# Experts' attention weights through DRAM: blocks of every fourth key, one transfer out and one back

## The chip, the cores and the metric

One core of one Trainium2 chip runs the whole program. The metric is the device time of one execution in microseconds; the median of three runs is compared. Beside the runs there is one profiled execution with a trace of every instruction. The engines are called PE (TensorE matmul), PEld (its weight loads), DVE (VectorE), ACT (ScalarE), POOL (GpSimd) and SP (SyncE, which here issues nearly all transfers).

## The reference

Three stages follow one another. The change touches the third alone.

```
attn_out = windowed attention with ALiBi over q, k, v             # B=4, H=8, S=576, D=64
x = transpose(attn_out) -> [4, 576, 512]
x = gated unit: relu(x @ w_in) -> u, v; v normalised, mixed over positions by w_spatial; (u * v) @ w_out
# third stage: mixture of 4 experts, each a causal attention of head size 64, top 2 of 4 by a gate
logits = x @ w_gate                    # [4, 576, 4]; softmax over the best two -> w
for e in range(4):
    q, k, v = x @ wq[e], x @ wk[e], x @ wv[e]
    scores = where(causal, -1e9, (q @ k.T) / 8)
    a = exp(scores - max); a /= a.sum(-1) + 1e-9
    ye = a @ v @ wo[e]
    out += (e is among the best two of this token) * w * ye
```

## The kernel before

**Tiling.** In the third stage a batch `b` (0 to 3) has 576 queries in five tiles `j`: four of 128 queries, and a tail (`j` = 4) of the last 64. For `j` below 4 the tile `(b, j)` holds 128 queries by the (j+1)·128 keys that they may see, for four experts `i`. For the tail, two experts stand in each half of the partitions, so that 64 queries fill 128 partitions; it sees all 576 keys. Positions are stored rolled by 64: columns 0 to 63 of the inputs are the tail's tokens, columns 64 to 575 the tokens 0 to 511.

**Steps of a tile.** The order of every step on every engine of the third stage is a list written out by hand, `THIRD`; the diff leaves it alone. Names in it are a kind and indices: `S` score matmuls into a PSUM bank pair (`scores_b`), `l` mask, scale and row minimum on DVE (`row_min`, which writes the tile's weights `p` in SBUF), `e` exponential and row sum on ACT, `f` the factors on DVE, `m` the scaling on POOL, `T` the turning of 32x32 blocks on DVE (`turn_blocks`, L1186), `w` the transfer of the turned weights to DRAM (`send`, L1193), `R` the transfer back (`read_back`, L1203), `A` the matmuls of values with turned weights (`attend_b`, L1239), `oh`/`ol` their removal from PSUM, `O` the output projection. `Q` and `qh`/`ql` are the projections of queries and keys and their removal, `V` and `vr` those of the values, `q4`/`k4` the tail's queries and keys in plain float32.

**Why DRAM.** Matmuls of values need the keys on the partitions. DVE turns each 32x32 block in place, so that after `T` the partition 32q + r holds, in block k, key 32k + r for the queries 32q to 32q + 31. What is left is a move of whole 32-row groups between partitions, and the way through DRAM does it. Before the change a block is 32 neighbouring keys: `send` issues four transfers, one for each group q of 32 partitions, in runs of 512 bytes (256 for the tail), into a DRAM tile ordered block, row, group. `read_back` then takes rows of 2048 bytes (1024 for the tail, in two transfers, of 128 and of 64 partitions). Three tiles, (3,2), (3,1) and (3,0), are turned on PE instead (`TURNED`).

**Buffers.** Banks for score pairs come from a pool of two (`psS`), all other PSUM banks from a pool of four (`psD`); a bank is free again when DVE's or ACT's last read of it has ended. `p` and the returned `pT` have three buffers each. Transfers of SP are issued in the order of its list, and each completion semaphore of eight is taken again only when the transfer that had it eight earlier has landed.

**Between the stages.** The masks `trit` (128 queries) and `tritail` (the tail) are made at the end of the second stage: POOL writes zeros, and SP loads the triangle beside them (L914 to L919). This stretch is not in a list by hand: the framework orders it by its own estimate of times. SP's list goes on there with the loads `st_wc` of the experts' weights `wcat` (L902) and `wt` (L957), from which PE makes the folded weights `W` for the third stage.

Of the kernel before, what the change touches and what calls it, by code (L numbers as in the profile page):

```python
# [10 lines left out]
F32 = mybir.dt.float32  # L11
BF16 = mybir.dt.bfloat16
# [6 lines left out]
ALU = mybir.AluOpType  # L19
# [3 lines left out]
B, H, S, D = 4, 8, 576, 64  # L23
P = 128
# [6 lines left out]
BIG = -float(2.0**40)  # L31
FAR = float(2.0**45)
FLT_MAX = 3.0e38
# [202 lines left out]
def block_kernel(ctx, tc, qP, kP, v, w_in, wspT, bsp, w_outT, wcat, wo, relt, tri, out):  # L236
    nc = tc.nc
# [10 lines left out]
    dram = ctx.enter_context(tc.tile_pool(name="dram", bufs=1, space=bass.MemoryType.DRAM))  # L248
# [663 lines left out]
    wB = ctx.enter_context(tc.tile_pool(name="wB", bufs=1, side="right", reuse_waits="tile"))  # L912
# [1 line left out]
    trit = wB.tile([P, 640], BF16, name="trit")  # L914
    nc.gpsimd.memset(trit[:, :512], 0.0)
    nc.sync.dma_start(trit[:, 512:640], tri[:, 0:128])
    tritail = wB.tile([P, S], BF16, name="tritail")
    nc.gpsimd.memset(tritail[:, :512], 0.0)
    nc.sync.dma_start(tritail[:, 512:576], tri[:, 128:192])  # L919
    tie = wB.tile([P, 1, E, E], F32, name="tie")  # L920
    nc.gpsimd.memset(tie, 0.0)
    for e in range(1, E):
# [91 lines left out]
    made = {}  # L1014

    def get(key, make):
        if key not in made:
            made[key] = make()
        return made[key]
# [11 lines left out]
    def values(b):  # L1031
        return get(("vt", b), lambda: wk.tile([P, 5, 260], F32, tag="vt", name=f"vt{b}"))
# [39 lines left out]
    def value_take(b, t):  # L1072
        pv = bank("pvB", b, t)
        if t < 4:
            nc.scalar.copy(values(b)[:, t, :], pv[:, :260])
        else:
            for o in range(2):
                nc.scalar.copy(values(b - 1 + o)[:64, 4, :], pv[64 * o : 64 * o + 64, :260])

    def gates(b, t0):  # L1080
        n = 1 if t0 else 4 + b % 2
# [25 lines left out]
    def tail_gate(b):  # L1107
        gt, gq = gate_of(b)
        for pr in range(2):
            nc.scalar.copy(gq[64 * pr : 64 * pr + 64, :], gt[0:64, 4, 2 * pr : 2 * pr + 2])  # L1110

    def keys_seen(j):
        return min(S, TOK[j][0] + P)
# [1 line left out]
    def score_bank(b, j, pr):  # L1115
        key = (b, j, 0 if j < 2 else pr)
        two = get(("psB", *key), lambda: psS.tile([P, 2, 512], F32, tag="S", name="psB%d_%d_%d" % key))
        return two[:, :, 256 * pr : 256 * pr + keys_seen(j)] if j < 2 else two

    def scores_b(b, j, at):  # L1120
        q0, kn = TOK[j][0], keys_seen(j)
        Q, K = heads(b, 0), heads(b, 1)
        if j == 4:
            view = score_bank(b, j, at)
            for c, k0, w in ((0, 64, 256),) if at == 0 else ((0, 320, 256), (256, 0, 64)):
                for pr in range(2):
                    for o in range(2):
                        r = slice(64 * o, 64 * o + 64)
                        nc.tensor.matmul(view[64 * pr : 64 * pr + 64, o, c : c + w], made["q4", b][r, pr, :], made["k4", b][r, pr, k0 : k0 + w], start=True, stop=True)
            return  # L1130
        for pr in (0, 1) if j < 2 else (at,):
            view = score_bank(b, j, pr)
            for n, (x_, y_) in enumerate(PASSES):
                for o in range(2):
                    r = slice(64 * o, 64 * o + 64)
                    nc.tensor.matmul(view[:, o, :kn], Q[x_][r, pr, 64 + q0 : 192 + q0], K[y_][r, pr, 64 : 64 + kn], start=(n == 0), stop=(n == 2))  # L1136

    def weights(b, j):
        n = 4 if j < 4 else 2
        p, st = get(("p", b, j), lambda: (wk.tile([P, 16 * P], F32, tag="p", name=f"pB{b}_{j}", bufs=3), wk.tile([P, 12], F32, tag="stat", name=f"stB{b}_{j}", bufs=4)))  # L1140
        if (b, j) in TURNED:
            return p, st, lambda i: p[:, i * (j + 1) * P : (i + 1) * (j + 1) * P], lambda t: t
        v = p[:, : (4 * (j + 1) if j < 4 else 18) * n * 32].rearrange("p (k e c) -> p k e c", e=n, c=32)
        return p, st, lambda i: v[:, :, i, :], lambda t: t.rearrange("p (k c) -> p k c", c=32)

    def row_min(b, j, i):
        p, st, part, cut = weights(b, j)
        V = nc.vector
        if j < 4:
            pr, o = divmod(i, 2)  # L1150
            q0, kn = TOK[j][0], keys_seen(j)
            V.tensor_tensor_reduce(part(i), cut(score_bank(b, j, pr)[:, o, :kn]), cut(trit[:, 512 - q0 : 512 - q0 + kn]), -0.125, FLT_MAX, ALU.add, ALU.min, st[:, i : i + 1])  # L1152
            return
        for n, (c0, w) in enumerate(((0, 256), (256, 320))):
            V.tensor_tensor_reduce(part(i)[:, c0 // 32 : (c0 + w) // 32], cut(score_bank(b, j, n)[:, i, :w]), cut(tritail[:, c0 : c0 + w]), -0.125, FLT_MAX, ALU.add, ALU.min, st[:, 8 + 2 * i + n : 9 + 2 * i + n])
        V.tensor_tensor(st[:, i : i + 1], st[:, 8 + 2 * i : 9 + 2 * i], st[:, 9 + 2 * i : 10 + 2 * i], op=ALU.min)

    def row_exp(b, j, i):
# [29 lines left out]
    def send(b, j):  # L1188
        p = weights(b, j)[0]
        n, w, e = sizes(j)  # L1190
        mid = get(("mid", b, j), lambda: dram.tile([16 if j < 4 else 18, 32, 4, w], F32, tag=f"mid{w}", name=f"mid{b}_{j}", bufs=3))
        for q in range(4):
            nc.sync.dma_start(mid[:n, :, q, :].rearrange("k i w -> i k w"), p[32 * q : 32 * q + 32, : n * w].rearrange("i (k w) -> i k w", w=w))  # L1193

    ready = {}

    def read_back(b, j):
        n, w, e = sizes(j)
        mid = made["mid", b, j]
        pT = wk.tile([P, 16 * P], F32, tag="pT", name=f"pTB{b}_{j}", bufs=3)  # L1200
        for c0, m, rows in ((0, n // 4, 128),) if j < 4 else ((0, 4, 128), (4, 1, 64)):
            src = mid[4 * c0 : 4 * c0 + rows // 32 * m].rearrange("(c k) i a w -> (k i) c (a w)", c=m)
            nc.sync.dma_start(pT[:rows, c0 * 4 * w : (c0 + m) * 4 * w].rearrange("i (c w) -> i c w", c=m), src)  # L1203
        full = pT[:, : (n + 3) // 4 * 4 * w].rearrange("p (c a e q) -> p c a e q", a=4, e=e, q=32)
        ready[b, j] = lambda pr, c, o: full[:, c, :, 2 * pr + o, :] if j < 4 else full[: 64 if c == 4 else 128, c, 2 * pr : 2 * pr + 2, o, :]

    homes = ["k0", "k1", "q0", "q1"]

# [22 lines left out]
    def attend_b(b, j):  # L1231
        qn = TOK[j][1]
        px = bank("pxB", b, j).rearrange("p (r c) -> p r c", r=4)
        vt, rhs = values(b), ready[b, j]
        for pr in range(2):
            for c in range(j + 1):
                kb = 64 if c == 4 else 128
                for o in range(2):
                    nc.tensor.matmul(px[64 * o : 64 * o + 64, pr, :qn], vt[:kb, c, (2 * pr + o) * 64 : (2 * pr + o) * 64 + 64], rhs(pr, c, o), start=(c == 0), stop=(c == j))  # L1239

    def take_b(b, j, part):
        qn = TOK[j][1]
# [35 lines left out]
    def act(name):  # L1278
        kind, rest_ = re.match(r"([a-zA-Z]+)(.*)$", name).groups()
        key = [int(k) for k in rest_.split(".")]  # L1280
        if kind in ("L", "GH", "GL", "BH", "BL"):
            load_g(name)
        elif kind == "VZ":
            nc.gpsimd.memset(values(*key)[64:128, 4, 256:260], 0.0)
        elif kind in ("qf", "kf"):
            whole(key[0], "qk".index(kind[0]), *key[1:])
        elif kind in ("qh", "ql"):
            project_take(*key, "hl".index(kind[1]))
        elif kind in ("oh", "ol"):
            take_b(*key, "hl".index(kind[1]))  # L1290
        elif kind == "g":
            get(("g", *key[:2]), lambda: gates(*key[:2]))[key[2]]()
        elif kind == "O":
            out_tile(*key[:2], key[-1], *key[2:-1])
        else:
            {"Q": project, "V": value, "vr": value_take, "h": tail_gate, "S": scores_b, "l": row_min, "e": row_exp, "f": factors, "m": scale, "T": turn_blocks,
             "w": send, "R": read_back, "t": turn_b, "c": turn_take, "A": attend_b, "oc": out_take, "o": out_store}[kind](*key)
# [11 lines left out]
def _tables():  # L1309
    import ml_dtypes  # L1310
    import numpy as np

    p = np.arange(128)[:, None]
    c = np.arange(256)[None, :]


    slope = -8.0 * 2.0 ** -(np.arange(H) + 1.0)[None, :, None]
    pair = [2 * np.arange(4) + (o ^ np.arange(4) % 2) for o in range(2)]
    tail = np.concatenate([slope[:, pair[o]] * ((p[:64] - c[:, :128]) % 128)[:, None, :] for o in range(2)], axis=0)
    tri = np.concatenate([np.where(c[:, :128] <= p, 0.0, BIG), np.where(c[:, :64] <= p % 64, 0.0, BIG)], axis=1)  # L1320
    return [t.astype(ml_dtypes.bfloat16) for t in (tail, tri)]


# [48 lines left out]
```

## Time and profile before

| | us |
|---|---|
| median of 3 runs (427.76 to 428.37) | 427.79 |
| profiled execution | 428.7 |
| span of its instructions | 426.8 |
| PE busy in the span | 411.0 |
| DVE busy | 316.6 |
| ACT busy | 243.1 |
| POOL busy | 171.2 |

The profiled execution has 1.9 us around its span, and is 0.9 us above the median. Its granted TensorE clock was 0.998 of full speed. The third stage begins at about 266 us of the span. A busy PE is not a PE at its peak: matmuls overlap, and their ends are modelled. Rows of a timeline or of a chain give start, length, and what ran; "[0.88 <-ACT u L780]" is idle time of the engine before the row and what ended it.

### The profile page before, as it was taken

To read this page: it belongs to the slowest core of one execution; us is meant where nothing else is said; L and a number is where in the kernel's file an instruction comes from. 1 tells how busy PE (TensorE), PEld (TensorE's weight loads), DVE (VectorE), ACT (ScalarE), POOL (GpSimd) and SP (SyncE) were. 2 spreads that over 40 slices of the span, in tenths; PEclk is the share of its full clock that TensorE was granted. 3 is DMA by queue.
4 is the path that set the end of the run, shared out by engine and by line. 5 is a ranking of instruction groups with operands and counts; after the bars stand their busy time and mean duration, and the time that the engine had idled before them with its cause. 6 is when DMAs were issued, how large, how long until landed. Compare 5 with 4: busy or idle time off the path is not lost.

```text
span 426.8 us, 12095 instructions
## 1 busy us (share of the span) xinstructions
PE 411.0 (96%) x4399; PEld 367.6 (86%) x4399; DVE 316.6 (74%) x1061; ACT 243.1 (57%) x757; POOL 171.2 (40%) x265
## 2 busy tenths in 40 slices
PE   6789999999999899999999999999999999999996
PEld 5567788799989798899898999999999998988885
DVE  5998999999899878787455422649888788678541
ACT  6898768756565455564245202656666557546642
POOL 3575553637406455432210000139665653544100
PEclk9999999999999999999999999999999999999999
DMA  8997366948855775331376160211879977798894
GB/s 249 382 298 287 101 170 206 293 127 259 274 171 134 220 231 156 90 104 39 118 256 263 49 223 2 63 50 26 217 198 282 248 160 244 214 270 219 204 279 126
DMA packets 76943, 80.06 MB, mean 188 GB/s; under 512 B 18002, under 2 KB 52946, under 8 KB 76500
## 3 DMA queue, kind: packets, MB, share of 16 engines
q1 hardware_dynamic: 76740, 79.15, 62.8%
q8 instruction: 35, 0.57, 0.6%
q14 instruction: 24, 0.20, 0.1%
q10 hardware_dynamic: 144, 0.13, 0.1%
HBM read 49.64 MB, written 29.62 MB: 186 GB/s over the span
## 4 chain that ended last, share of the span: by engine, by line
PE 77%; DMA 10%; DVE 4%; SPq 3%; ACT 3%; issue 1%; POOL 1%; DVEq 0%; POOLq 0%; ACTq 0%
PE pq L1042 12%; PE pu L777 10%; PE pg L792 9%; PE pv L714 9%; PE pvB L1070 6%; PE pxB L1239 6%; PE pout_None L1257 6%; PE psB L1136 4%; PE pw L946 4%; PE px L679 2%; DMA v<-in_v 2%; DMA carry<-p 2%; PE px L650 2%; DMA reltail<-in_relt 2%; DMA st_wc<-in_wcat 1%; DMA raw<-in_w_in 1%
## 5 line engine op out<-in xcount | busy, mean ns | idle before, releaser
L286 ACT ACTIVATE p<-p,st 128x128 f32<-128x128 f32 x144 | 56.5, 396 | 23.8 <-DVE st L285 19.3
L792 PE MATMUL pg<-wsp,vn 128*128 128x288 f32 x384 | 60.3, 297 | 0.9 <-ACT u L780 0.9
L777 PE MATMUL pu<-x,win 128*128 128x288 f32 x384 | 58.0, 297 | 0.2 <-DVE g L800 0.2
L714 PE MATMUL pv<-win,x 128*128 128x512 f32 x216 | 57.3, 398 | 0.3 <-ACT x L700 0.3
L792 PEld LDWEIGHTS pg<-wsp,vn 128*128 128x128 f32 x384 | 54.2, 188 | 3.4 <-ACT u L780 1.3
L565 POOL TENSOR_TENSOR p<-p,st 128x512 f32<-128x512 f32 (+1 forms) x28 | 32.4, 1162 | 60.9 <-DVE st L563 29.2
L1042 PE MATMUL pq<-x,W 128*128 128x288 f32 x384 | 56.8, 297 | 0.0
L777 PEld LDWEIGHTS pu<-x,win 128*128 128x128 f32 x384 | 53.4, 188 | 2.9 <-issue 1.0
L1042 PEld LDWEIGHTS pq<-x,W 128*128 128x128 f32 x384 | 52.5, 188 | 1.6 <-issue 0.8
L1160 ACT ACTIVATE pB<-pB,stB 128x128 f32<-128x128 f32 (+4 forms) x72 | 41.7, 581 | 13.8 <-DVE stB L1152 6.3
L298 POOL TENSOR_SCALAR pB<-pB,stB 128x384 f32<-128x384 f32 (+4 forms) x64 | 35.9, 580 | 28.8 <-DVE stB L1169 14.3
L714 PEld LDWEIGHTS pv<-win,x 128*128 128x128 f32 x216 | 38.4, 188 | 8.4 <-ACT x L700 1.2
L1152 DVE CUSTOM_DVE_ANT_0 pB<-psB,trit 128x128 f32<-128x128 f32 (+3 forms) x64 | 27.9, 485 | 6.0 <-PE psB L1136 5.7
L285 DVE CUSTOM_DVE_ANT_0 p<-ps,relm 128x128 f32<-128x128 f32 x128 | 30.1, 281 | 1.8 <-DMA carry<-p 1.7
L602 POOL TENSOR_SCALAR_AFFINE_SELECT pU<-pT 128x512 f32<-128x512 f32 (+1 forms) x26 | 18.8, 730 | 23.7 <-DMA pT<-carry 23.5
L1186 DVE STREAM_TRANSPOSE pB<-pB 128x1024 f32<-128x1024 f32 (+3 forms) x28 | 26.9, 980 | 1.9 <-POOL pB L298 1.7
L286 ACT ACTIVATION_READ_ACCUMULATOR p<-p,st 128x1 f32 x144 | 27.5, 191 | 0.0
L1070 PE MATMUL pvB<-W,x 128*128 128x260 f32 x192 | 27.1, 284 | 0.0
L1239 PE MATMUL pxB<-pTB,vt 128*64 128x128 f32 (+2 forms) x480 | 26.4, 260 | 0.0
L1257 PE MATMUL pout_None<-wo,o 128*128 128x512 f32 x102 | 26.3, 401 | 0.0
L1239 PEld LDWEIGHTS pxB<-pTB,vt 128*64 128x64 f32 (+1 forms) x480 | 23.2, 136 | 2.8 <-issue 1.1
L1070 PEld LDWEIGHTS pvB<-W,x 128*128 128x128 f32 x192 | 24.7, 188 | 0.8 <-issue 0.7
(195 smaller groups left out, 932.7 us busy)
## 6 DMA issues: line engine op xcount, KB each, us to landing
carry<-p SPq DMA_DIRECT2D x96, 64.0 KB, 2.4
pT<-carry SPq DMA_DIRECT2D x24, 256.0 KB, 3.1
q<-in_qP SPq DMA_DIRECT2D x20, 256.0 KB, 3.4
g_dram<-g SPq DMA_DIRECT2D x16, 288.0 KB, 3.8
gf<-g_dram SPq DMA_DIRECT2D x16, 288.0 KB, 4.8
raw<-in_w_in SPq DMA_DIRECT2D x8, 512.0 KB, 6.3
v<-in_v SPq DMA_DIRECT2D x16, 256.0 KB, 5.2
mid<-pB SPq DMA_DIRECT2D x16, 256.0 KB, 4.8
```

What stands on the lines that cost most here:

```text
L285: lambda: nc.vector.tensor_tensor_reduce(s_view, ps_view, tab, -0.125, FLT_MAX, ALU.add, ALU.min, nm),
L286: lambda: nc.scalar.activation(s_view, s_view, AF.Exp, bias=nm, scale=-1.0, accum_out=sm),
L298: nc.gpsimd.tensor_scalar(p, p, r, 0.0, op0=ALU.mult, op1=ALU.add)
L565: ops["m"] = lambda: nc.gpsimd.tensor_tensor(blocks, blocks, sm.unsqueeze(1).unsqueeze(3).to_broadcast([P, 4, n, 32]), op=ALU.mult)
L714: nc.tensor.matmul(pv, x[i][:, k, t0 : t0 + P], win[j][:, k, 512:1024], start=(n == 0 and k == 0), stop=(n == 2 and k == 3))
L777: nc.tensor.matmul(pu[:, :HALF], win[i][:, k, m * P : (m + 1) * P], x[j][:, k, c], start=(n == 0 and k == 0), stop=(n == 2 and k == 3))
L792: nc.tensor.matmul(pg[:, :HALF], vn[i][k][:, m * P : (m + 1) * P], wsp[j][:, k, c], start=(n == 0 and k == 0), stop=False)
L1042: nc.tensor.matmul(pq[:, :HALF], W[i][c0 // CUT][:, k, c0 % CUT : c0 % CUT + P], G[j][:, k, c], start=(n == k == 0), stop=(n == 2 and k == 3))
L1070: nc.tensor.matmul(pv[:, :260], rows, W[j][1][:, k, 512 - CUT :], start=(n == k == 0), stop=(n == 2 and k == 3))
L1160: nc.scalar.activation(part(i), part(i), AF.Exp, bias=st[:, i : i + 1], scale=-1.0, accum_out=st[:, 4 + i : 5 + i])
L1239: nc.tensor.matmul(px[64 * o : 64 * o + 64, pr, :qn], vt[:kb, c, (2 * pr + o) * 64 : (2 * pr + o) * 64 + 64], rhs(pr, c, o), start=(c == 0 ...
L1257: nc.tensor.matmul(po[:, : c.stop - c.start], o2[i][:, pr, :], wos[j][:, pr, c], start=(n == pr == 0), stop=(n == 2 and pr == 1))
```

## The change

A block becomes 32 keys of which each is four after the last (two in the tail), so that the partition of the returned tile is the row within the block times four (two) plus the block's residue. `send` is then one transfer of whole rows of the weights tile, and `read_back` one transfer (two for the tail) that takes, for each partition and group q, a run of (j+1)·512 bytes. For the tiles of 128 queries the reordering is made by `row_min`, which reads scores and mask in steps of four elements. For the tail it is made by `scores_b`, whose matmuls read the keys in steps of two elements, in 16 matmuls where there were 12. The tail's values move to the upper half of the partitions. The DRAM tiles get a tag for each `j` and four buffers.

```diff
-    tritail = wB.tile([P, S], BF16, name="tritail")
-    nc.gpsimd.memset(tritail[:, :512], 0.0)
-    nc.sync.dma_start(tritail[:, 512:576], tri[:, 128:192])
+    tritail = wB.tile([P, 2, 288], BF16, name="tritail")
+    nc.gpsimd.memset(tritail, 0.0)
+    nc.sync.dma_start(tritail[:, :, :32], tri[:, 128:192].rearrange("p (z i) -> p z i", z=2))
...  value_take
-                nc.scalar.copy(values(b - 1 + o)[:64, 4, :], pv[64 * o : 64 * o + 64, :260])
+                nc.scalar.copy(values(b - 1 + o)[64:, 4, :], pv[64 * o : 64 * o + 64, :260])
...  tail_gate
-            nc.scalar.copy(gq[64 * pr : 64 * pr + 64, :], gt[0:64, 4, 2 * pr : 2 * pr + 2])
+            nc.scalar.copy(gq[64 * pr : 64 * pr + 64, :], gt[64:128, 4, 2 * pr : 2 * pr + 2])
...  scores_b, j == 4
-            for c, k0, w in ((0, 64, 256),) if at == 0 else ((0, 320, 256), (256, 0, 64)):
+            for y, c, n in ((0, 0, 5), (1, 160, 4)):
                 for pr in range(2):
                     for o in range(2):
                         r = slice(64 * o, 64 * o + 64)
-                        nc.tensor.matmul(view[64 * pr : 64 * pr + 64, o, c : c + w], made["q4", b][r, pr, :], made["k4", b][r, pr, k0 : k0 + w], start=True, stop=True)
+                        keys = made["k4", b][r, pr, :].rearrange("p (g i z) -> p g i z", i=32, z=2)[:, y:9:2, :, at]
+                        to = view[64 * pr : 64 * pr + 64, o, c : c + 32 * n].rearrange("p (g i) -> p g i", i=32)
+                        nc.tensor.matmul(to, made["q4", b][r, pr, :], keys, start=True, stop=True)
...  weights
-        return p, st, lambda i: v[:, :, i, :], lambda t: t.rearrange("p (k c) -> p k c", c=32)
+        return p, st, lambda i: v[:, :, i, :], lambda t: t.rearrange("p (c z) -> p z c", z=4)
...  row_min, j == 4
-        for n, (c0, w) in enumerate(((0, 256), (256, 320))):
-            V.tensor_tensor_reduce(part(i)[:, c0 // 32 : (c0 + w) // 32], cut(score_bank(b, j, n)[:, i, :w]), cut(tritail[:, c0 : c0 + w]), ...)
+        for n in range(2):
+            V.tensor_tensor_reduce(part(i)[:, 9 * n : 9 * n + 9], score_bank(b, j, n)[:, i, :288], tritail[:, n, :], ...)
...  send
-        mid = get(("mid", b, j), lambda: dram.tile([16 if j < 4 else 18, 32, 4, w], F32, tag=f"mid{w}", name=f"mid{b}_{j}", bufs=3))
-        for q in range(4):
-            nc.sync.dma_start(mid[:n, :, q, :].rearrange("k i w -> i k w"), p[32 * q : 32 * q + 32, : n * w].rearrange("i (k w) -> i k w", w=w))
+        mid = get(("mid", b, j), lambda: dram.tile([P, n * w], F32, tag=f"mid{j}", name=f"mid{b}_{j}", bufs=B))
+        nc.sync.dma_start(mid, p[:, : n * w])
...  read_back
-        mid = made["mid", b, j]
+        src = made["mid", b, j].rearrange("(q i) (z c) -> (i z) q c", q=4, z=e)
-        for c0, m, rows in ((0, n // 4, 128),) if j < 4 else ((0, 4, 128), (4, 1, 64)):
-            src = mid[4 * c0 : 4 * c0 + rows // 32 * m].rearrange("(c k) i a w -> (k i) c (a w)", c=m)
-            nc.sync.dma_start(pT[:rows, c0 * 4 * w : (c0 + m) * 4 * w].rearrange("i (c w) -> i c w", c=m), src)
-        full = pT[:, : (n + 3) // 4 * 4 * w].rearrange("p (c a e q) -> p c a e q", a=4, e=e, q=32)
+        if j < 4:
+            nc.sync.dma_start(pT[:, : n * w].rearrange("p (q c) -> p q c", q=4), src)
+        else:
+            to = pT[:, : 20 * w].rearrange("p (q c) -> p q c", q=4)
+            nc.sync.dma_start(to[64:], src[:, :, : 5 * w])
+            nc.sync.dma_start(to[:64, :, w:], src[:, :, 5 * w :])
+        full = pT[:, : (n + 2 if j == 4 else n) * w].rearrange("p (a c e q) -> p c a e q", a=4, e=e, q=32)
...  attend_b: the tail's fifth chunk reads partitions 64 to 127 instead of 0 to 63, the same matmuls otherwise
```

## Rows read from the trace of the kernel before

**Rows 1.** Page, busy time: share of the span, instructions.

```profile
PE 411.0 (96%) x4399; PEld 367.6 (86%) x4399; DVE 316.6 (74%) x1061; ACT 243.1 (57%) x757; POOL 171.2 (40%) x265
```

**Rows 2.** Chain that ended last, 266 to 345 us, then 345 to 427: start, length, what.

```profile
by line: PE pq L1042 52.5%; PE pvB L1070 24.2%; PE psB L1136 11.3%; PE pxB L1239 8.1%; PE psB L1129 2.9%; PE pw L946 1.1%
...
305.65 1.14 PE psB L1129 x24
...
by line: PE pout_None L1257 30.4%; PE pxB L1239 23.4%; PE pq L1042 13.2%; PE psB L1136 10.7%; PE pvB L1070 9.8%; PE ptB L1218 3.2%; PE psB L1129 2.6%; PE pout L1257 1.7%; ACT ot L1265 0.5%; issue 0.0%; ACTq L1265 0.0%
...
417.49 2.34 PE pxB L1239 x48
```

**Rows 3.** Waits of SP's queue, 250 us to the end: us in total, times, longest.

```profile
SPq L1193 <- DVE pB L1186: 29.7, 9, 18.3
...
SPq L1203 <- DMA mid<-pB: 7.6, 8, 2.8
```

**Rows 4.** DMA issues: count, KB each, median us to landing.

```profile
mid<-pB SPq DMA_DIRECT2D x16, 256.0 KB, 4.8
...
pTB<-mid SPq DMA_DIRECT2D x7, 512.0 KB, 5.5
```

**Rows 5.** The DRAM tile's transfers on SP: duration ns min/median/max, first and last start.

```profile
L1193 SPq DMA_DIRECT2D mid<-pB x68: 303/492/3607, 294.3 to 404.1; - x68
L1203 SPq DMA_DIRECT2D pTB<-mid x21: 365/531/1682, 301.0 to 412.2; - x21
```

**Rows 6.** Timeline of SP near the end: start, length, what.

```profile
410.94 1.75 SPq L1203 DMA_DIRECT2D pTB<-mid  x2
```

**Rows 7.** Groups by line and form, DVE, third stage: busy us, mean ns.

```profile
L1152 DVE CUSTOM_DVE_ANT_0 pB<-psB,trit 128x512 f32<-128x512 f32 x16 | 10.3, 684 | 0.9 <-PE psB L1136 0.8
...
L1152 DVE CUSTOM_DVE_ANT_0 pB<-psB,trit 128x128 f32<-128x128 f32 x16 | 3.8, 286 | 0.4 <-PE psB L1136 0.3
```

**Rows 8.** One line of the first stage (word_ops "or"): duration ns min/median/max.

```profile
L440 DVE SCALAR_TENSOR_TENSOR u<-raw,u x8: 660/691/1385, 6.6 to 44.6; 128x512 int32<-128x512 int32 x8
```

**Rows 9.** Stretches of 10 us: busy PE, PEld, DVE, ACT, POOL, then clock and DMA.

```profile
290.00:300.00 10.00, 10.00 (x82) 9.17 (x79) 9.02 (x33) 5.64 (x19) 9.26 (x19) 1.00 0.22 45
...
320.00:330.00 10.00, 10.00 (x107) 9.07 (x104) 8.40 (x30) 6.33 (x21) 5.72 (x10) 1.00 0.99 287
...
350.00:360.00 10.00, 10.00 (x82) 8.65 (x80) 8.57 (x36) 7.86 (x26) 4.25 (x10) 1.00 0.93 261
```

**Rows 10.** The same stretches, DVE's instructions of L1152 alone.

```profile
290.00:300.00 10.00, 3.10 (x14) 1.00 0.22 45
...
320.00:330.00 10.00, 3.85 (x15) 1.00 0.99 287
...
350.00:360.00 10.00, 5.20 (x23) 1.00 0.93 261
```

**Rows 11.** A bank's way from DVE to PE: timelines of DVE and of PE.

```profile
303.30 0.42 DVE L263 TENSOR_TENSOR q<-pq,q 128x288 fp32r<-128x288 f32 x1
...
305.02 0.63 PE L1070 MATMUL pvB<-W,x 128*128 128x260 f32 x4
```

**Rows 12.** The tail's scores: L1129 in stretches (PE, PEld); then PE's groups, 306.16 to 306.19.

```profile
305.57:305.84 0.27, 0.26 (x4) 0.21 (x8) 1.00 1.03 273
...
L1129 PE MATMUL psB<-k,q 64*64 64x64 f32 x8 | 0.3, 217 | 0.0
```

**Rows 13.** Between the stages: timelines of SP, POOL and PE.

```profile
214.45 0.43 SPq L919 DMA_DIRECT2D tritail<-in_tri  x1
214.93 0.91 SPq L902 DMA_DIRECT2D st_wc<-in_wcat  x2
...
214.51 0.54 POOL L918 MEMSET tritail<- 128x512 bf16 x1
...
234.17 1.33 PE L792 MATMUL pg<-wsp,vn 128*128 128x288 f32 x8 [0.88 <-ACT u L780]
```

**Rows 14.** Chain that ended last, 226 to 250 us.

```profile
226.81 6.14 DMA st_wc<-in_wcat
```

More of the change, by code (lines that the diff above doesn't have):

```diff
@@ L1153, in row_min @@
             return
-        for n, (c0, w) in enumerate(((0, 256), (256, 320))):
-            V.tensor_tensor_reduce(part(i)[:, c0 // 32 : (c0 + w) // 32], cut(score_bank(b, j, n)[:, i, :w]), cut(tritail[:, c0 : c0 + w]), -0.125, FLT_MAX, ALU.add, ALU.min, st[:, 8 + 2 * i + n : 9 + 2 * i + n])
+        for n in range(2):
+            V.tensor_tensor_reduce(part(i)[:, 9 * n : 9 * n + 9], score_bank(b, j, n)[:, i, :288], tritail[:, n, :], -0.125, FLT_MAX, ALU.add, ALU.min, st[:, 8 + 2 * i + n : 9 + 2 * i + n])
         V.tensor_tensor(st[:, i : i + 1], st[:, 8 + 2 * i : 9 + 2 * i], st[:, 9 + 2 * i : 10 + 2 * i], op=ALU.min)
@@ L1198, in read_back @@
         n, w, e = sizes(j)
-        mid = made["mid", b, j]
+        src = made["mid", b, j].rearrange("(q i) (z c) -> (i z) q c", q=4, z=e)
         pT = wk.tile([P, 16 * P], F32, tag="pT", name=f"pTB{b}_{j}", bufs=3)
-        for c0, m, rows in ((0, n // 4, 128),) if j < 4 else ((0, 4, 128), (4, 1, 64)):
-            src = mid[4 * c0 : 4 * c0 + rows // 32 * m].rearrange("(c k) i a w -> (k i) c (a w)", c=m)
-            nc.sync.dma_start(pT[:rows, c0 * 4 * w : (c0 + m) * 4 * w].rearrange("i (c w) -> i c w", c=m), src)
-        full = pT[:, : (n + 3) // 4 * 4 * w].rearrange("p (c a e q) -> p c a e q", a=4, e=e, q=32)
-        ready[b, j] = lambda pr, c, o: full[:, c, :, 2 * pr + o, :] if j < 4 else full[: 64 if c == 4 else 128, c, 2 * pr : 2 * pr + 2, o, :]
+        if j < 4:
[5 more added lines that the diff above has]
+        full = pT[:, : (n + 2 if j == 4 else n) * w].rearrange("p (a c e q) -> p c a e q", a=4, e=e, q=32)
+        ready[b, j] = lambda pr, c, o: full[:, c, :, 2 * pr + o, :] if j < 4 else full[64 if c == 4 else 0 :, (c + 1) % 5, 2 * pr : 2 * pr + 2, o, :]
     homes = ["k0", "k1", "q0", "q1"]
@@ L1236, in attend_b @@
             for c in range(j + 1):
-                kb = 64 if c == 4 else 128
+                kb = slice(64 if c == 4 else 0, P)
                 for o in range(2):
-                    nc.tensor.matmul(px[64 * o : 64 * o + 64, pr, :qn], vt[:kb, c, (2 * pr + o) * 64 : (2 * pr + o) * 64 + 64], rhs(pr, c, o), start=(c == 0), stop=(c == j))
+                    nc.tensor.matmul(px[64 * o : 64 * o + 64, pr, :qn], vt[kb, c, (2 * pr + o) * 64 : (2 * pr + o) * 64 + 64], rhs(pr, c, o), start=(c == 0), stop=(c == j))
     def take_b(b, j, part):
@@ L1283, in act @@
         elif kind == "VZ":
-            nc.gpsimd.memset(values(*key)[64:128, 4, 256:260], 0.0)
+            nc.gpsimd.memset(values(*key)[0:64, 4, 256:260], 0.0)
         elif kind in ("qf", "kf"):
@@ L1319, in _tables @@
     tail = np.concatenate([slope[:, pair[o]] * ((p[:64] - c[:, :128]) % 128)[:, None, :] for o in range(2)], axis=0)
-    tri = np.concatenate([np.where(c[:, :128] <= p, 0.0, BIG), np.where(c[:, :64] <= p % 64, 0.0, BIG)], axis=1)
+    tri = np.concatenate([np.where(c[:, :128] <= p, 0.0, BIG), np.where(2 * (c[:, :64] % 32) + c[:, :64] // 32 <= p % 64, 0.0, BIG)], axis=1)
     return [t.astype(ml_dtypes.bfloat16) for t in (tail, tri)]
```

## The prediction, made before the changed kernel ran

> **What bounds the kernel now.** I read the busy times first, then the chain of work that ended last, then the waits of SP's queue, and last the groups of instructions that the diff touches. The busy times name PE, 411.0 of 426.8 us [rows 1]. An average hides stages, so the chain decides: from 266 to 345 us it consists of PE rows alone, and from 345 to the end of PE rows but for half a per cent [rows 2]. No transfer of the weights stands in it, in either stretch. The reader is to see there that the third stage is as long as PE's list of matmuls, and that a change in it is worth what it adds to or takes from that list, plus any wait that it brings up into it.
>
> SP's queue does wait, 29.7 us for DVE's turned blocks and 7.6 us for the weights to land in DRAM before they are fetched [rows 3]. That is time in which SP has nothing else ready to issue. It would count if PE waited for what is fetched, so the distance between fetch and use is the next thing to look at. The tightest is the last tile, (3,4): its two fetches are issued from 410.94 us on in 1.75 us [rows 6], the larger form of such a fetch lands after 5.5 us in the median [rows 4], so about 416.5 us, and the stretch of matmuls that opens with its own begins at 417.49 [rows 2]. There is about 1 us to spare in the worst place. Faster transfers make that 1 us larger and give PE nothing.
>
> **Transfers.** 17 tiles are sent with 4 issues each, 68 in all, with a median of 492 ns on SP [rows 5]; 51 go away, some 25 us of SP's time. The write changes from runs of 512 and 256 bytes to whole rows, the read from 2048 bytes to (j+1)·512. Packets fall for j = 3 from 2048 + 512 to 128 rows + 512, and for j = 0 stay at 640. So landing gets shorter, by an unknown part of the 4.8 us that a quarter of the largest tile takes [rows 4]. Worth on the path: 0, because PE's list covers it, at the tightest by the 1 us above. If a new transfer were longer than the old by more than that, PE would stop at the last tile by the rest; with the same bytes in fewer issues I see no ground for that.
>
> **Row minima, tiles of 128 queries.** 13 tiles keep this way, 52 instructions of L1152, with the same columns; what changes is that scores in PSUM are read in steps of four floats (16 bytes) and the mask in steps of 8 bytes. [...] No instruction before the change reads PSUM in such steps. The nearest row is L440, which reads SBUF in steps of two words (8 bytes) with 512 columns: 691 ns [rows 8], against 684 for 512 columns read without gaps. Lower bound: nothing. Upper bound: each column costs twice. [...] I take nothing, since the one strided row cost nothing, and keep the other end as a rival.
>
> [...]
>
> **Tail, row minima.** Two instructions of 256 and 320 columns become two of 288, now read without gaps: 576 columns either way. 0.
>
> **Tail, scores.** The columns stay 576 for each expert; three pieces become four, so a batch has 32 records where it had 24 (each float32 matmul shows as two). A batch takes 1.14 us now [rows 2]. Upper bound, if a record costs the average whatever its length: 8 · 1.14/24 = 0.38 us a batch, 1.5 us for four. Lower bound: nothing, if columns alone count. The rows are near the lower: four records of 256 columns, which run together, fill 0.27 us before a fifth begins, while all eight records of 64 columns are under way together with later ones [rows 12], so short records follow at a small part of the average. I take 0.1 us for four batches. This is on PE's list, with nothing to hide it. The keys are also read in steps of 8 bytes. Nothing on PE did that before; the bounds are nothing and a doubling of the four batches, 4 · 1.14 = 4.6 us. L440's row says that 8 bytes cost DVE nothing, and I take nothing, with the doubling as a rival.
>
> **Values of the tail, its gates, the zeroed columns.** The same instructions on other partitions: 0. The returned tile is read by `attend_b` in runs of 32 as before: 0.
>
> **The tail's mask.** Before, POOL zeroed 512 columns while SP loaded 64 others; the load was issued at 214.45 us, inside POOL's 214.51 + 0.54 [rows 13]. Now the load goes into the zeroed columns and has to wait for POOL, till about 215.1 us. What stands behind it in SP's list are the loads `st_wc` and `wt`, and a later `st_wc` stands in the chain with 6.14 us [rows 14]; PE idles 0.88 us before 234.17 us because of it [rows 13]. So this small edit lies closer to the path than the transfers do. If SP's order stays, everything behind moves by 215.15 - 214.45 = 0.7 us, and so does PE. If the framework, which orders this stretch by its own estimate, lets the two `st_wc` go first, they start 0.48 us earlier, and PE gets up to that back. Two ends, +0.7 and -0.5; I see no row that leans to either and take their middle, +0.1.
>
> **Sum.** 0 + 0 + 0.1 + 0.1 = +0.2 us. The profiled execution would go from 428.7 to 428.9; it stands 0.9 above the median of the runs, so in the runs' terms 427.79 + 0.2 = 428.0, from 427.2 to 428.6 with the two ends of the mask's wait and some of the tail's.
>
> **Rivals.** *DVE reads PSUM at half speed in steps of 16 bytes* (slower). Of an instruction of 512 columns, 0.53 of 0.684 us are columns, 0.78 of it, which doubling adds once more: 2.4 us to 290-300, 3.0 to 320-330, 4.1 to 350-360 [rows 10]. DVE has 9.02, 8.40 and 8.57 of 10 us taken there [rows 9], so it overruns by 1.4, 1.4 and 2.7 us, and the stretches in between are too full to recover the first. A bank that PE wants at 305.02 us was freed by DVE at 303.72 [rows 11]: 1.3 us of slack, and DVE's lag passes it from about 300 us on. PE then waits for banks. The overruns sum to 5.5 us; slack takes some off, the crowding of minima within a stretch adds some; I put it at 6, so 434. It decides as soon as a column costs more than about half as much again, since up to there the lag stays within the slack. For it: the largest of DVE's loads lie in the tightest stretches. Against it: 8 bytes cost nothing.
>
> *PE reads keys at half speed in steps of 8 bytes* (slower): up to +4.6 us, 0.2 with it, so about 432. Four tail batches would show it at once, and nothing else.
>
> *The mask's load moves behind `st_wc` and the lighter SP queue brings up more* (faster): at the most the whole idle 0.88 us before 234.17, so 426.9. For it: PE does idle there for a transfer. Against it: only the first transfers move, by 0.48.
>
> *The transfers don't get shorter at all*: 428.0 too, as nothing on the path waits for them.
>
> **How the numbers follow.** For this kernel 0.2% (0.86 us) is about what a measurement tells from no change. No change, 427.2 to 428.6: 0.50. DVE at half speed, 430.5 to 436, likeliest 434: 0.27. PE at half speed, 430 to 432.5: 0.13. Faster, 426.5 to 427: 0.10. The first gives "same"; the second and third "slower", 0.40; the fourth "faster". The predicted time is the likeliest, 428.0. A range that leaves out no more than 2 in 10 has to take in both slower cases in part: 427.0 to 434.5 holds 0.50 + 0.13 + about 0.18. The likeliest case's own range is 427.2 to 428.6.
>
> **What the profile after would show.** Row minima of 512 columns near 684 ns confirm the first step; near 1,200 they show the rival, with PE waiting for banks from 300 us on. A tail batch of 1.1 to 1.2 us confirms the second; 2 us the rival. SP's issue of the tail's mask at 215.1, or behind `st_wc`, settles the third, and PE's idle before its matmuls near 234 us says what it cost. Sends should be 17, and the fetch of (3,4) should land more than 1 us before its matmuls. What would make the prediction wrong is a strided read that costs more than the one at 8 bytes, or a wait in the third stage that no view of the kernel before shows.

## The result, and the profile after

The changed kernel takes 430.58 us in the median of four runs (430.28 to 431.4), the kernel before 428.02 in four runs beside it: a ratio of 1.0062 with a 95% interval from 1.0045 to 1.008. A second comparison, of 12 runs with 23 (`after_again` below), gives 1.0046 [1.0028, 1.0065]. It is slower by about 2 to 2.6 us. The time lies inside the range of 427.0 to 434.5, but the likeliest case was "no change", and that did not come. The profiled execution takes 430.81 us and its span is 428.8, at a granted clock of 0.999.

The busy times on the page answer to [rows 1]:

```profile
PE 410.8 (96%) x4431; PEld 368.2 (86%) x4431; DVE 316.6 (74%) x1061; ACT 243.6 (57%) x757; POOL 169.3 (39%) x265
```

PE has 32 records more (four batches with 8 each) and is busy for 410.8 us against 411.0, although the span is 2.0 us longer. So the loss is idle time of PE. DVE is busy for the same 316.6 us, so the row minima did not become slower. The groups of the row minima on DVE (line, form, then busy us and mean ns of one) answer to [rows 7]:

```profile
L1154 DVE CUSTOM_DVE_ANT_1 pB<-psB,trit 128x512 f32<-128x512 f32 x16 | 10.4, 685 | 0.8 <-PE psB L1138 0.8
...
L1154 DVE CUSTOM_DVE_ANT_1 pB<-psB,trit 128x128 f32<-128x128 f32 x12 | 2.8, 285 | 0.3 <-PE psB L1138 0.3
```

685 and 285 ns stand against 684 and 286. The transfers, as DMA issues with KB each and median us to landing, answer to [rows 4]; SP's issues of the sends (ns min/median/max) to [rows 5]:

```profile
mid<-pB SPq DMA_DIRECT2D x4, 1024.0 KB, 4.8
...
pTB<-mid SPq DMA_DIRECT2D x4, 1024.0 KB, 6.1
...
pTB<-mid SPq DMA_DIRECT2D x4, 320.0 KB, 6.4
```

```profile
L1194 SPq DMA_DIRECT2D mid<-pB x17: 319/325/390, 296.0 to 402.5; - x17
```

One transfer of 1 MB lands in the 4.8 us that a quarter of it took before. The packets of the whole program fall from 76,943 to 53,854, by the page. The chain from 266 to 345 us and from 345 us on still consists of PE's rows; the tail's scores in it, and the last matmuls that wait for a fetch, answer to [rows 2] and [rows 6]:

```profile
307.32 1.19 PE psB L1131 x30
...
340.27 1.19 PE psB L1131 x32
...
392.45 1.20 PE psB L1131 x31
...
419.35 2.34 PE pxB L1243 x48
```

```profile
411.61 0.58 SPq L1206 DMA_DIRECT2D pTB<-mid  x1
```

A batch of tail scores takes 1.19 us instead of 1.14. Of the last tile's two fetches the larger is issued at 411.61 us; each of its kind landed after 6.4 us, so it lands at 418.0, 1.3 us ahead of its matmuls. The smaller is issued at 412.25 and lands, by the median of its own kind (6.1 us), about 1.0 us ahead of them.

Then PE's waits from 205 to 262 us, between the stages. First the kernel before, then the changed one (us in total, times, longest):

```profile
PE pg L792 <- ACT u L780: 0.9, 1, 0.9
```

```profile
PE pv L714 <- DVE g L800: 2.3, 1, 2.3
```

That is the place of the loss. The wait of [rows 13] before 234 us is gone, and a longer one has come, for a gate product `g` on DVE. The timelines of SP and of DVE show how:

```profile
214.31 0.33 SPq L916 DMA_DIRECT2D trit<-in_tri  x1
214.69 0.91 SPq L902 DMA_DIRECT2D st_wc<-in_wcat  x2
215.64 0.43 SPq L919 DMA_DIRECT2D tritail<-in_tri  x1
```

```profile
218.82 0.96 DVE L263 TENSOR_TENSOR wc<-st_wc,wc 128x772 fp32r<-128x772 f32 x1 [1.81 <-ACT wc L266]
219.71 0.45 DVE L800 TENSOR_TENSOR g<-u,pg 128x288 f32<-128x288 f32 x1
```

The same stretch of DVE in the kernel before:

```profile
216.69 0.45 DVE L800 TENSOR_TENSOR g<-u,pg 128x288 f32<-128x288 f32 x1
218.93 2.07 DVE L263 TENSOR_TENSOR wc<-st_wc,wc 128x772 fp32r<-128x772 f32 x2 [1.79 <-ACT wc L266]
```

The framework let the two `st_wc` go ahead of the tail's mask, and in the same stroke it put the step of the folding that needs them (`wc`, the low part of a chunk) ahead of `g` on DVE. DVE ran them in that order: `g`, which ran at 216.69 us before, waits for `wc`, which waits for ACT's cast of the same chunk, which waits for the transfer. By the kernel `g` is the last to read its PSUM bank, and the banks that PE's next matmuls `pv` need come from the same pool; so PE stops. The chain of the changed kernel runs through it:

```profile
214.69 3.25 DMA st_wc<-in_wcat
217.96 0.84 ACT wc L266
218.82 0.96 DVE wc L263
219.78 0.38 DVE g L800
220.21 1.19 PE pv L714 x4
```

POOL's zeroing of `trit` begins between 211.62 and 214.29 us in the profiles of this study, a spread that arises ahead of what the change touches. So I compare stretches that begin there and last to the end of the span. It starts at 214.05 us before and at 214.29 after:

```profile
214.05 0.53 POOL L915 MEMSET trit<- 128x512 bf16 x1 [4.55 <-PE py L679]
```

```profile
214.29 0.53 POOL L915 MEMSET trit<- 128x512 bf16 x1 [4.15 <-PE py L679]
```

Before: 426.8 - 214.05 = 212.75 us. After: 428.8 - 214.29 = 214.51, so 1.76 more. PE's waits account for 2.3 - 0.9 = 1.4 of it and the tail's scores for 4 · 0.05 = 0.2; 0.16 are left without a name, less than two profiles of one kernel differ by.

### The profile page after: what moved, and what is told of

Same layout as the page of the kernel before. It is cut to its first block, busy times and chain, and to the rows that moved or that the text cites. A ratio compares the mean times of both kernels' runs of the same rounds, so it can differ in the third digit from the quotient of the medians.

```text
span 428.8 us, 12019 instructions
## 1 busy us (share of the span) xinstructions
PE 410.8 (96%) x4431; PEld 368.2 (86%) x4431; DVE 316.6 (74%) x1061; ACT 243.6 (57%) x757; POOL 169.3 (39%) x265
## 2 busy tenths in 40 slices
DMA packets 53854, 80.04 MB, mean 187 GB/s; under 512 B 8098, under 2 KB 29986, under 8 KB 52900
## 4 chain that ended last, share of the span: by engine, by line
PE 74%; DMA 13%; ACT 4%; DVE 4%; SPq 2%; issue 1%; POOL 0%; DVEq 0%; ACTq 0%
PE pq L1042 12%; PE pg L792 9%; PE pu L777 9%; PE pv L714 7%; PE pvB L1070 6%; PE pxB L1243 6%; PE pout_None L1261 6%; PE psB L1138 4%; PE pw L946 4%; DMA carry<-p 3%; DMA raw<-in_w_in 3%; DMA v<-in_v 2%; PE px L679 2%; ACT p L286 2%; DMA k<-in_kP 2%; PE pg L795 2%
## 5 line engine op out<-in xcount | busy, mean ns | idle before, releaser
L602 POOL TENSOR_SCALAR_AFFINE_SELECT pU<-pT 128x512 f32<-128x512 f32 (+1 forms) x26 | 17.4, 678 | 25.2 <-DMA pT<-carry 25.1
L1154 DVE CUSTOM_DVE_ANT_1 pB<-psB,trit 128x512 f32<-128x512 f32 (+3 forms) x52 | 23.6, 501 | 1.9 <-PE psB L1138 1.9
```

## Experiments

Times of the kernel before differ a little between sets of runs, so each ratio is to its own. The ratio is the recorded one and not the quotient of two medians. "Stretch" is the time from the zeroing of `trit` to the end of the span, in the one profiled execution. Two profiles of the same kernel differ there by 0.24 to 0.53 us (the changed kernel and `after_again`, the two of `before_mask_waits`, the two `late_fold` runs), so differences of 0.2 us in that column show nothing by themselves.

| run | median us | ratio to before [95%] | stretch us | PE's waits, 205 to 262 us |
|---|---|---|---|---|
| kernel before | 427.39 to 428.02 | | 212.75 | 0.9 for `u` |
| changed kernel | 430.58 | 1.0062 [1.0045, 1.008] | 214.51 | 2.3 for `g` |
| mask_apart | 427.81 | 1.0003 [0.9991, 1.0014] | 212.98 | 0.9 for `u` |
| before_mask_waits | 429.50 | 1.005 [1.0029, 1.0071] | 214.27 | 2.2 for `g` |
| fold_low_on_pool | 430.12 | 1.0059 [1.0037, 1.0082] | 216.21 | 2.4 for `u` |
| four_sends | 427.53 | 0.9996 [0.9978, 1.0014] | 212.68 | 0.8 for `u` |
| masks_later | 427.58 | 1.0003 [0.9987, 1.0018] | 212.61 | 0.5 for `g` |
| late_fold_on_pool | 426.88 | 1.0001 [0.9986, 1.0017] | 211.91 | none |
| tail_keys_in_order | 427.54 | 1.001 [0.9993, 1.0027] | 212.82 | 0.9 for `u` |
| minima_in_order | 427.44 | 1.0002 [0.9987, 1.0016] | 213.18 | 0.9 for `u` |
| late_fold_again | 427.18 | 0.9984 [0.9967, 1.0002] | 212.44 | 0.3 for `u` |
| before_late_fold | 426.28 | 0.9966 [0.9951, 0.998] | 211.78 | none |
| after_again | 429.50 | 1.0046 [1.0028, 1.0065] | 214.75 | 2.0 for `g`, 0.4 for `u` |
| before_mask_waits_again | 429.66 | 1.005 [1.0029, 1.0071] | 214.58 | 2.1 for `g`, 0.5 for `u` |

The theory was that the whole loss comes from one line, the zeroing of the tail's mask, by way of the order that the framework then chooses. The rivals were that the layout costs (transfers, strided reads), and that the wait of the mask's load costs as such.

**mask_apart.** The changed kernel, with POOL's zeros kept off the columns that SP loads:

```diff
-    nc.gpsimd.memset(tritail, 0.0)
+    nc.gpsimd.memset(tritail[:, :, 32:], 0.0)
```

> The changed kernel, but POOL zeroes only the columns of the tail's mask that the load does not fill, so the load waits for nothing. Theory: the loss arises between the stages, because the waiting load lets the framework put a step of the weights' folding ahead of a gate product on DVE; with the wait gone that order returns and the time is that of before plus the tail's scores, 428.0 + 0.2 = 428.2 us, with PE's idle before its matmuls near 234 us back at 0.9. Rival: the loss lies in the new layout of the third stage (strided reads, new transfers); then the time stays at 430.6.

The loss is gone. SP, DVE and PE's waits are as they were before the change:

```profile
213.24 0.33 SPq L916 DMA_DIRECT2D trit<-in_tri  x1
213.62 0.43 SPq L919 DMA_DIRECT2D tritail<-in_tri  x1
214.09 0.95 SPq L902 DMA_DIRECT2D st_wc<-in_wcat  x2
```

```profile
215.86 0.45 DVE L800 TENSOR_TENSOR g<-u,pg 128x288 f32<-128x288 f32 x1
218.34 2.02 DVE L263 TENSOR_TENSOR wc<-st_wc,wc 128x772 fp32r<-128x772 f32 x2 [2.04 <-ACT wc L266]
```

All of the change but this line costs about 0.2 us of the stretch (212.98 against 212.75), which is within the scatter, and nothing that the runs can tell.

**before_mask_waits.** The reverse: the kernel before, with nothing but the zeroing changed, so that its load must wait too.

```diff
-    nc.gpsimd.memset(tritail[:, :512], 0.0)
+    nc.gpsimd.memset(tritail, 0.0)
```

> The kernel before, with one word changed: POOL zeroes all 576 columns of the tail's mask, so the load into the last 64 has to wait for it. Nothing of the layout or the transfers changes. Theory: it loses what the changed kernel lost between the stages, 1.4 to 2.4 us, 429.4 to 430.4 us, and DVE again turns to the folding before the gate product at about 217 us. Rival (the layout is the cause): 428.0, no change.

The loss is there without any part of the layout, by the same order on DVE:

```profile
217.83 0.96 DVE L263 TENSOR_TENSOR wc<-st_wc,wc 128x772 fp32r<-128x772 f32 x1 [1.68 <-ACT wc L266]
218.71 0.45 DVE L800 TENSOR_TENSOR g<-u,pg 128x288 f32<-128x288 f32 x1
```

Its stretch is 1.52 us longer than before, against the changed kernel's 1.76. The two runs settle that the one line is enough for the loss, and that the loss goes with it.

**four_sends.** `mask_apart` with four sends for each tile, in whole rows of 32 partitions:

```diff
-        nc.sync.dma_start(mid, p[:, : n * w])
+        for q in range(4):
+            nc.sync.dma_start(mid[32 * q : 32 * q + 32], p[32 * q : 32 * q + 32, : n * w])
```

> The version with the mask's load free of the wait, but each tile goes to DRAM in four transfers of 32 partitions as before the change, in the new layout. Theory: transfers are covered by PE's list, so this is within 0.3 us of that version with one transfer, about 428.2. Rival: the single transfer saves something on PE's way, and four cost 0.5 us or more.

The time is that of `mask_apart` as far as the runs can tell, and so are the stretch and PE's wait. One issue instead of four is worth nothing here that shows.

**fold_low_on_pool.** The changed kernel, with the low parts of the two chunks of the folding that are loaded first made on POOL, so that DVE has nothing to wait for.

```diff
-        return lambda: split(wc[0][k], wc[1][k], raw_[k])
+        def halves():
+            nc.scalar.copy(wc[0][k], raw_[k])
+            lo_part(wc[1][k], raw_[k], wc[0][k], nc.gpsimd if k >= 2 else nc.vector)
+        return halves
```

> The changed kernel with its waiting mask, but the low parts of the two weight chunks that are loaded first are made on POOL and not on DVE. Theory: what cost time is that a gate product stood on DVE behind a step that waited for a transfer; with that step off DVE the product runs at about 217 us again, PE's wait of 2.3 us for it goes, and the time is 427.3 to 428.3. Rival that the waiting transfers themselves delay PE, not the order on DVE: 430 or more. Rival that the layout is the cause: 430.6.

This missed. `g` is early again, at 215.53 us, and PE's wait for it is gone; but PE now waits 2.4 us for `u`. The chain from 214 to 236 us says why:

```profile
222.29 6.70 DMA gf<-g_dram
229.08 0.40 ACT both L990
...
230.00 0.32 ACT u L780
...
231.54 0.96 PE pu L777 x4
```

ACT stands at `both`, a cast of the next stage's input, until the transfer `gf` lands at 229.0 us, and `u` stands behind it. It is the same kind of wait on another engine. In the kernel before ACT runs this `u` at 227.91 us, ahead of `both`. In the changed kernel it stands behind `both`, as here; but PE is late there by its wait for `g`, and `both` waits only 0.25 us:

```profile
230.04 0.41 ACT L986 CAST both<-gf 128x256 fp32r<-128x256 f32 x1 [0.25 <-DMA gf<-g_dram]
```

So the new order held a second wait, hidden behind the first, and taking one blocked instruction off one engine brought it up. It also shows again in `after_again` and `before_mask_waits_again`, as 0.4 and 0.5 us for `u`.

The stretch is 1.70 us longer than the changed kernel's, at nearly the same length of wait. The chain shows where: just after the 2.4 us in which PE waited, it has these rows:

```profile
230.37 1.17 PE pg L792 x4
231.54 0.96 PE pu L777 x4
232.50 0.96 PE pg L792 x4
233.46 0.82 PE pu L777 x4
234.28 1.06 PE pg L792 x8
```

The 16 matmuls from 230.37 to 234.28 us take 3.91 us, 0.82 to 1.17 for a group of four; the eight after them take 1.06, so 0.53 for a group, as in the kernel before (229.01 to 229.54 us). At 0.53 us a group the 16 would have taken 2.12, so they cost some 1.8 us. That a lower granted clock made them slow is my estimate: the mean granted clock of this execution is 0.991, against 0.999 in the profiled one of the changed kernel. The changed kernel's trace has nothing of the kind after its 2.31 us of waiting: its granted clock is 1.00 from 220 to 225 us. How often other executions had such a slow place is open.

**masks_later.** This tells the wait from the order. `mask_apart`, with the loads of both masks issued after those of `wt`:

```diff
-    nc.sync.dma_start(trit[:, 512:640], tri[:, 0:128])
...
-    nc.sync.dma_start(tritail[:, :, :32], tri[:, 128:192].rearrange("p (z i) -> p z i", z=2))
...
             nc.sync.dma_start(wt[i][:, k, :].bitcast(F32), wt_dram[i, k])
+    nc.sync.dma_start(trit[:, 512:640], tri[:, 0:128])
+    nc.sync.dma_start(tritail[:, :, :32], tri[:, 128:192].rearrange("p (z i) -> p z i", z=2))
```

> The changed kernel with the tail's mask zeroed in the upper part alone, so that its load waits for nothing, and with the loads of both masks moved behind the loads of wt. The two st_wc then go first on SP, some 0.9 us earlier than where the masks stand ahead. Theory (the order costs, not the wait): the framework again puts the step wc of the folding ahead of the gate product g on DVE, PE waits for g for about 1.9 us (2.3 less the 0.4 that st_wc comes earlier than in the changed kernel), and the 0.9 us of idle before 234 us go away: 428.5 to 429.5, although no load waits for POOL. Rival (the wait of the mask's load costs): nothing waits now, so 427.8 or less, and g stands ahead of wc.

The order came as the theory said, the time did not: 0.5 us of waiting in place of 1.9. My figure took the `st_wc` to start near 213 us, where the masks had started. The timelines of SP and DVE show what I had not seen:

```profile
204.02 0.97 SPq L902 DMA_DIRECT2D st_wc<-in_wcat  x2
205.03 5.86 SPq L955 DMA_DIRECT2D wt<-wt_dram  x8
...
217.86 0.35 SPq L956 DMA_DIRECT2D trit<-in_tri  x1
```

```profile
216.06 0.96 DVE L263 TENSOR_TENSOR wc<-st_wc,wc 128x772 fp32r<-128x772 f32 x1
216.94 0.45 DVE L800 TENSOR_TENSOR g<-u,pg 128x288 f32<-128x288 f32 x1
```

The `st_wc` go at 204.02 us, some ten earlier. In the other kernels the load of `trit` holds SP's queue till about 213 us; SP's waits show that it stands there for PE's matmuls `py` of the first stage (the row is from the kernel before):

```profile
SPq L916 <- PE py L679: 9.3, 1, 9.3
```

So `wc` ahead of `g` costs 2.3 us while its transfer is late, and only its own 0.9 us on DVE, 0.5 of them seen by PE, when the transfer has landed. The order and the late transfer make the loss together. `wc` again stands ahead of `g` here and the runs show no loss, so the rival's time of 427.8 or less came without its reason.

**late_fold_on_pool and late_fold_again.** A try at a faster version. In the kernel before, and in `mask_apart`, PE loses 0.9 us near 233 us because `u` stands on ACT behind two casts of late chunks. ACT's timeline in `mask_apart`:

```profile
231.12 1.78 ACT L266 CAST wc<-st_wc 128x772 fp32r<-128x772 f32 x2 [0.92 <-DMA st_wc<-in_wcat]
232.80 0.40 ACT L780 ACTIVATE u<-pu 128x288 f32<-128x288 f32 x1
```

The edit gives POOL, which is idle there, the cast and the low part of these two chunks (on top of `mask_apart`):

```diff
-        return lambda: split(wc[0][k], wc[1][k], raw_[k])
+        def halves():
+            (nc.gpsimd.tensor_copy if k < 2 else nc.scalar.copy)(wc[0][k], raw_[k])
+            lo_part(wc[1][k], raw_[k], wc[0][k], nc.gpsimd if k < 2 else nc.vector)
+        return halves
```

> The changed kernel with the tail's mask zeroed in the upper part alone, and the two late chunks of the folding (cast and low part) made on POOL in place of ACT and DVE. A try at a version that is faster than both. If PE's idle 0.9 us near 233 us comes from u standing on ACT behind two casts that wait for st_wc, it goes away: 426.9 to 427.2 in runs where the kernel before has 427.9. If something else comes last there (the gate product on DVE, the matmuls pu), PE waits for that in the same place and the time stays at 427.8. POOL needs some 6 us for the two chunks and the folding's matmuls begin about 12 us later, so they should not be late.

> The same kernel as late_fold_on_pool, for a second measurement of its time. By its profile PE waits nowhere from 205 to 262 us, and from the memset of trit (211.99 us) to the end of the span it takes 211.9 us, against 212.75 in the kernel before (214.05 to 426.8): a ratio of 0.998. Theory: 0.997 to 0.999 of the kernel before. Rival (the 0.9 us come back elsewhere or go under in what the first stage varies): 1.000.

The wait is gone in the first profile and 0.3 us of it is left in the second. POOL's row:

```profile
229.93 1.79 POOL L936 CAST wc<-st_wc 128x772 fp32r<-128x772 f32 x2 [0.44 <-DMA st_wc<-in_wcat]
231.68 3.69 POOL L263 TENSOR_TENSOR wc<-st_wc,wc 128x772 fp32r<-128x772 f32 x2
```

The two measurements give 1.0001 and 0.9984, and both intervals hold 1: whether this version with the change beats the kernel before is not settled by them.

**before_late_fold.** The same edit on the kernel before, without any of the change.

> The kernel before with the two late chunks of the folding made on POOL, without anything of the change. Theory (PE's 0.9 us of idle before 234 us come from u behind two casts on ACT, whatever the change does): PE waits nowhere there, 211.7 us from the memset of trit to the end of the span, 0.2 less than with the change, as the tail scores are at 1.14 us; ratio 0.997 to 0.999. Rival: the order shifts again and the wait comes back at another place, ratio 1.000 or above.

0.9966 [0.9951, 0.998]: faster, at 426.28 us against 427.79, a little more than the theory's 0.997 to 0.999. The stretch is 0.97 us shorter than before; PE waits nowhere in it. It is the only kernel here whose interval lies below 1, it was measured once, and its interval overlaps that of `late_fold_again`. It needs nothing of the change.

**tail_keys_in_order.** `mask_apart` with the tail's keys read without steps, in the same four pieces; the kernel leaves out the new order of the tail's keys:

```diff
-                        keys = made["k4", b][r, pr, :].rearrange("p (g i z) -> p g i z", i=32, z=2)[:, y:9:2, :, at]
+                        k0 = 288 * at + c
+                        keys = made["k4", b][r, pr, k0 : k0 + 32 * n].rearrange("p (g i) -> p g i", i=32)
```

> The changed kernel with the tail's mask zeroed in the upper part alone, and the keys of the tail's scores read without steps, in the same four pieces; this leaves out the turning of the tail's keys. Theory (the step of 8 bytes costs PE nothing, the rest of the 0.05 us a batch is the two more pieces): a batch of tail scores stays at 1.19 us and the time at 427.8. Rival (the step is what costs): a batch goes back to 1.14 us, 0.2 us in all; PE at half speed in such steps would have shown 2.2 us in the changed kernel and can be seen there already.

The rival was right. The chain from 300 us on has the old 1.14 us for a batch, with all 32 records, and the groups differ by some ns a record; first this kernel, then the changed one:

```profile
305.38 1.14 PE psB L1132 x32
```

```profile
L1132 PE MATMUL psB<-k,q 64*64 64x160 f32 x64 | 3.9, 307 | 0.0
L1132 PE MATMUL psB<-k,q 64*64 64x128 f32 x64 | 3.4, 269 | 0.0
```

```profile
L1131 PE MATMUL psB<-k,q 64*64 64x160 f32 x64 | 4.1, 312 | 0.0
L1131 PE MATMUL psB<-k,q 64*64 64x128 f32 x64 | 3.5, 272 | 0.0
```

The additional records cost nothing that shows, and the step of 8 bytes costs 0.05 us a batch.

**minima_in_order.** `mask_apart` with scores and mask read without steps by the row minima of the tiles of 128 queries; the kernel leaves out the new order of their keys:

```diff
-        return p, st, lambda i: v[:, :, i, :], lambda t: t.rearrange("p (c z) -> p z c", z=4)
+        return p, st, lambda i: v[:, :, i, :], lambda t: t.rearrange("p (z c) -> p z c", z=4)
```

> The changed kernel with the tail's mask zeroed in the upper part alone, and the row minima reading scores and mask without steps; this leaves out the turning of the keys within blocks. Theory (steps of 16 bytes in PSUM cost DVE nothing): an instruction of 512 columns stays at 684 to 685 ns, the time at 427.8. Rival (part of the price is hidden in the 685): it falls to 670 ns or less, with the time still at 427.8, as the engine has some slack.

```profile
L1154 DVE CUSTOM_DVE_ANT_0 pB<-psB,trit 128x512 f32<-128x512 f32 x16 | 10.4, 684 | 0.8 <-PE psB L1138 0.8
```

684 ns, as with steps of 16 bytes. No part of the price was hidden in the 685.

**after_again and before_mask_waits_again.** The changed kernel and `before_mask_waits` once more, for the size of the loss.

> The changed kernel as it is, once more, for the size of its loss: its profile accounts for 1.76 us from the memset of trit to the end of the span (214.51 against 212.75 us), of which 0.2 are the tail's scores; the first comparison of medians gave 2.56 us from four runs of each. If the trace has the whole loss, the ratio comes out at 1.0035 to 1.005; if something ahead of that stretch is slower too, at 1.006 or above.

> The kernel before with the whole mask zeroed ahead of its load, once more and beside the changed kernel: 0.2 us below it if the tail's scores are all that the two differ by on PE's list (ratio to the kernel before 1.003 to 1.0045); as much as the first time, 1.005, if the runs of that time were typical.

1.0046 and 1.005 are one and the same within their intervals. By the first of them the loss is 2.0 us, with an interval from 1.2 to 2.8, which holds the 1.76 of the trace; nothing ahead of the stretch is needed to explain it. The 0.2 us that were expected between the two kernels can't be seen in the runs; in the stretches of this pair it is 0.17, within the scatter.

## Why the prediction was right or wrong

**Bound: right.** The third stage is as long as PE's list, and no transfer of the weights came into the chain.

**Transfers, 0: right.** They became shorter by the measure of packets (76,943 to 53,854) and of SP's issues (68 sends to 17), and the time did not notice (`mask_apart`, `four_sends`). The spare time at the last tile was put at about 1 us and is 1.0 to 1.3.

**Row minima, 0 against +6 us: right**, and for the reason given, that strided rows on DVE cost nothing: the row minima read PSUM in steps of 16 bytes, and 512 columns took 685 ns against 684 with neighbouring elements (`minima_in_order`). A column cost (684 - 286) / 384 = 1.04 ns before the change [rows 7] and (685 - 285) / 384 = 1.04 ns after it. For 512 columns that is 0.53 us, the part of an instruction that the rival with the slower DVE took twice.

**Tail's row minima, values and gates, 0:** nothing of them shows in the stretch of `mask_apart`, whose 0.2 us the tail's scores would fill.

**Tail's scores, +0.1: right in kind, mis-sized and put on the wrong half.** It is +0.2 for four batches. I gave the 0.1 to the additional records and nothing to the step of 8 bytes; it is the other way round (1.14 us a batch with all 32 records but without the step, 1.19 with it). Since the doubling did not come, the rival with PE at half speed falls.

**The tail's mask, +0.1: the step that failed.** The prediction saw that this small edit lies closer to the path than the transfers, and that the framework might let the two `st_wc` go first. It did, and they go 0.48 us earlier after the zeroing of `trit` (214.69 - 214.29 against 214.93 - 214.05), as worked out. The idle 0.88 us before 234 us went away too, but not by "PE gets up to that back": ACT's two late casts end only 0.25 us earlier (233.56 against 233.81), while PE, held up by the wait for `g`, reaches this place later, and the `u` behind the casts now waits for PE:

```profile
234.26 0.41 ACT L780 ACTIVATE u<-pu 128x288 f32<-128x288 f32 x1 [0.70 <-PE pu L777]
```

What the step left out is that an order chosen anew is chosen for all engines. It priced SP's list alone; on DVE `wc` went ahead of `g`, and PE paid 2.3 us there. The two ends of -0.5 and +0.7 did not hold +1.4, and their middle had no row to lean on.

**Rivals.** None of them was what happened: slower came, but not by DVE's or PE's reads. The faster rival's first step took place, the mask's load behind `st_wc`, and was outweighed by a wait that none of them had. That the range held the time is luck: it reached that far for cases that did not occur.

Why the framework moves `wc` ahead of `g` can't be read from a trace. That it goes by its estimate of when `st_wc` lands is an argument only; what is shown is that the order turns over with the one line: put into the kernel before, and taken out of the changed kernel.

## What to carry to other kernels

Where a framework orders a stretch by its own estimate, a small new wait is priced by the whole new order, on every engine, and not by the length of the wait: compare the instruction lists of all engines before and after, and look for an instruction on the path that now stands behind one that waits for a transfer, as `g` did here behind `wc` (2.3 us for PE). A second such place can hide behind the first, as `u` did behind `both` (2.4 us in `fold_low_on_pool`). When PE stops in such a place, the cure is the late transfer or the engine that waits for it. Here an idle POOL could take the work (-0.34%, measured once in the kernel before), and a load that nobody needed soon, `trit`, had held back a queue for 9.3 us.

## What the runs showed of the hardware

DVE read PSUM in steps of 16 bytes at the price of neighbouring elements (685 against 684 ns for 512 columns). PE's matmuls in float32 read their moving keys in steps of 8 bytes at 1 to 2% more for a record (312 against 307 ns for 160 columns, 272 against 269 for 128), and eight more records with the same columns cost nothing (1.14 us a batch with 24 and with 32). In `fold_low_on_pool` 16 matmuls after a wait of 2.4 us took 3.91 us, where at 0.53 us for four they would have taken 2.12; after an idle time of 2.31 us in the changed kernel the granted clock was 1.00. A transfer of 1 MB in rows of the whole tile landed in 4.8 us in the median, as long as a quarter of it had taken when four went out in runs of 512 bytes; with the four quarters sent as whole rows (`four_sends`), one of 256 KB took 4.2:

```profile
mid<-pB SPq DMA_DIRECT2D x16, 256.0 KB, 4.2
```
